# A mixer kernel on one Trainium2 core: batch 3's feature maps between the product reads of batch 1's block, and batch 0's last reads in another order

## The chip, the cores and the metric

The kernel runs on one core of a Trainium2 chip (trn2). The time is device microseconds (us) of one execution. Several runs are taken, and the median is given. Beside them there is one profiled execution, from which all rows of the trace come.

## What is computed

Eight batches of linear attention (8 heads, 576 positions, head size 64) are followed by a token-and-channel mixer.

```
phi(x) = where(x > 0, x, exp(x) - 1) + 1
kv = phi(k)^T v        z = sum over positions of phi(k)          per head
x  = (phi(q) kv) / (phi(q) z + 1e-6)                             576 x 512 per batch
u  = x + (relu(x^T w_tok1) w_tok2)^T                             token mixing, 576 -> 256 -> 576
out = u + relu(u w_ch1) w_ch2                                    channel mixing, 512 -> 1536 -> 512
```

Inputs and output are 32-bit floats. The matrix work inside is done in bfloat16.

## The kernel before, in words

**Tiling.** A batch has 576 positions: four row blocks of 128 and a tail of 64. The tails of two batches, 2p and 2p+1, share one block of 128 rows. The loaded q, k and v of a batch lie in `raw` buffers of two sets. Even batches and every batch from 2 on use set 0 and batch 1 uses set 1. After batch 1 the buffers of set 1 hold other things: sums of weights (`tb`, `tf`), sums of rows of the hidden layer (`sb`), and one of three parts of the output sum (`part`).

**One batch, stage by stage.**

- *Feature map.* phi is built as min(exp(x), max(x + 1, 1)). ScalarE does the exponential (`phi_exp`, L148), VectorE the add and max (`phi_add`, L154, into one of two buffers `y`) and the minimum (`phi_end`, L162, into `qp` or `kp`). Each step comes as two instructions of 128 x 1152, one for each half of the heads. The two ends of k are what `kv` (L188) waits for, with the cast of v (`vcast`, L173).
- *kv* is 72 small matmuls (L188). ScalarE copies the result out (L194). q is transposed by SyncE's transposing transfers (`qtr_dma`, L218).
- *Normalisation* (`nd_all`, L258 on TensorE; L267, L269, L271, L278 on VectorE) divides and gives x. It uses PSUM banks 2 to 7.
- *Token mixing* is `mm1` (L302, relu on ScalarE at L305) and `mm2` (L315). mm2 has two halves: mm2a gives rows 0 and 1 of u, mm2b rows 2 and 3. VectorE adds x (L327). Two transposing transfers on SyncE's queue (`utr_dma`, L510; called uta and utb) turn u into uT.
- *Channel mixing, first half* (`mm3`, L528) takes uT and makes the hidden layer `cr`, 12 column blocks of four matmuls. Each block has a PSUM bank that a tuple at L524 to L526 names. ScalarE (L535) or VectorE (L532) takes the relu. `mm3_tail` (L542, L544) does the same for the shared tail rows in three groups, with banks from the tuple at L538.
- *Channel mixing, second half.* Batches 1 to 6 use seven products in place of eight (`pair_product`, L690). A batch has 14 product steps (7 products, each for two row pairs) of 6 matmuls. The products are summed in three PSUM tiles X, Z and Y. Some need row sums of the hidden layer, which VectorE makes (`row_sums`, L625). ScalarE copies intermediate values of a tile out (`pair_copy`, L695). VectorE reads the tiles and adds u into the output buffer (`pair_end`, L701). GpSimd adds the copied parts (L703) and sends the result (L707). The tail rows are one product with `crt` (`mm4` with t = 8, L555, twelve matmuls).
- Batch 0 has no such products. Its second half (`mm4`, L555) sums in four held banks, t = 0 to 3, which the ring of banks puts in banks 2, 3, 0, 1. `mm4_end` (L572) reads each, adds u, and has GpSimd send two at a time (L577).

**Order.** Nothing is scheduled by a planner. The order on each engine is the order in which the program issues instructions. A block of batch n is a list `big` of steps of TensorE work, and a list `fill` of pairs (step, work), where the work is issued right after its step. In this way the work of batch n+1 (attention, token mixing) and the feature maps of batch n+2 stand between the matmuls of batch n. In batch 1's block, steps 0 to 11 are mm3, 12 to 14 mm3_tail, 15 to 28 the product steps, and 29 to 31 the tail product in groups of four matmuls. The products go in the order 1, 2, 6, 5, 7, 3, 4, so product step 17 is the first half of product 2, and 23 and 24 are product 7. kv of batch 3 stands behind step 29. Batch 2's block follows. It starts with mm3 of batch 2, which needs the whole of its uT.

**Queues.** SyncE's queue carries all loads (`load_all`, L129) and all transposing transfers in program order. A transfer that waits holds those behind it. GpSimd makes sums of weights early in batch 1's block (`weight_sums`, L611).

**Lines the change touches.** `mm3` L524 to L526, `mm3_tail` L538, `pair_product` L679, `pair_end` L697, the last `fill` of batch 0's block at L911 to L914, and the `put` list of batch 1's block at L931 to L975.

Of the kernel before, what the change touches and what calls it, by code (L numbers as in the profile page):

```python
# [18 lines left out]
def kernel(  # L19
# [26 lines left out]
    R = 4  # L46
# [18 lines left out]
    def bank(at=None):  # L65
        if at is None:
            at, ring[1] = ring[1], (ring[1] + 1) % 4
        return psum[:, at]
# [68 lines left out]
    live = {}  # L137
    o_at = [0]

    def o_slots(m):  # L140
        at = o_at[0] if o_at[0] + m <= 10 else 0
        o_at[0] = (at + m) % 10
        return obuf[:, at:at + m]
# [198 lines left out]
    def mm2_half(n, c):  # L342
        b = n % 2
        cs = COLS[c]
        for rs in ([0, 1], [2, 3]):
            ps = bank(4 + 2 * c + rs[0] // 2).rearrange(
                "p (r c) -> p r c", r=2)
            add = rs[0] == 0
            for i, r in enumerate(rs):
                if add:  # L350
                    nc.tensor.matmul(out=ps[:, i], lhsT=identity, rhs=x[b][:, r, cs],
                                     start=True, stop=False)
                for kt in range(NT):
                    nc.tensor.matmul(out=ps[:, i], lhsT=w2v(kt, r), rhs=ar[b][:, kt, cs],
                                     start=(kt == 0 and not add), stop=(kt == NT - 1))
            if add:
                nc.scalar.copy(out=u[b][:, 0:2, cs], in_=ps)
            else:
                nc.vector.tensor_tensor(out=u[b][:, 2:4, cs], in0=ps, in1=x[b][:, 2:4, cs],
                                        op=ALU.add)  # L360

    def utr(n, js):
        b = n % 2
        for jp in js:
            tp = bank(4 + 2 * jp).bitcast(BF16).rearrange("p (j r c) -> p j r c", j=2, r=R)
            for i in range(2):
                j = 2 * jp + i
                for r in range(R):
                    nc.tensor.transpose(out=tp[:, i, r, :],
                                        in_=u[b][:, r, 128 * j:128 * j + 128], identity=identity)  # L370
            for i, copy in enumerate((nc.scalar.copy, nc.vector.tensor_copy)):
                copy(out=uT[b][:, :, 2 * jp + i], in_=tp[:, i])
# [147 lines left out]
    def mm3(n, mc, kjs=range(NDM), dve=False):  # L520
        b = n % 2
        if kjs[0] == 0:
            part_of[mc] = bank(None if n == 0 else (
                (0, 1, 0, 1, 2, 3, 0, 1, 2, 3, 0, 1) if n > 1 else  # L524
                (3, 5, 7, 1, 3, 0, 2, 1, 3, 0, 1, 0))[mc])
        ps = part_of[mc]  # L526
        for kj in kjs:
            nc.tensor.matmul(out=ps, lhsT=wc1[:, kj, 128 * mc:128 * mc + 128],  # L528
                             rhs=uT[b][:, :, kj],
                             start=(kj == 0), stop=(kj == NDM - 1))  # L530
        if kjs[-1] == NDM - 1 and dve:
            nc.vector.tensor_scalar(out=cr[b][:, mc, :], in0=ps, scalar1=0.0, scalar2=None,  # L532
                                    op0=ALU.max)
        elif kjs[-1] == NDM - 1:
            nc.scalar.activation(out=cr[b][:, mc, :], in_=ps, func=AF.Relu)  # L535

    def mm3_tail(i, late=True):
        ps = bank(((2, 3, 0) if late else (1, 2, 3))[i]).rearrange("p (m s) -> p m s", m=4)  # L538
        for m in range(4):
            mc = 4 * i + m  # L540
            for kj in range(NDM):
                nc.tensor.matmul(out=ps[:, m], lhsT=wc1[:, kj, 128 * mc:128 * mc + 128],  # L542
                                 rhs=uTt[:, kj, :], start=(kj == 0), stop=(kj == NDM - 1))
        nc.scalar.activation(out=crt[:, 4 * i:4 * i + 4, :], in_=ps, func=AF.Relu)  # L544
# [18 lines left out]
    def mm4_end(p, t):  # L563
        ps = held[t]
        b, r = divmod(t, R)
        last = p == B // 2 - 1
        put = nc.sync if last else nc.gpsimd
        if t < 8:
            if last or r % 2 == 0:
                live["o"] = o_slots(2)  # L570
            o = live["o"][:, 0 if last else r % 2]
            nc.vector.tensor_tensor(out=o, in0=ps, in1=u[b][:, r, :], op=ALU.add)  # L572
            m = 1 if last else 2
            if r % m == m - 1:
                r0 = r - m + 1
                for e in range(2):
                    (nc.scalar if last and e else put).dma_start(  # L577
                        out=outv[2 * p + b, :, 2 * r0 + e:2 * r0 + e + 2 * m - 1:2],
                        in_=live["o"][half[e], 0:m])
        else:  # L580
            o = o_slots(2)[:, 0]
            nc.vector.tensor_tensor(out=o, in0=ps, in1=ut[p % 2], op=ALU.add)
            for b in range(2):
                (nc.scalar if last and b else put).dma_start(
                    out=outv[2 * p + b, :, 2 * R], in_=o[half[b]])
# [3 lines left out]
    KH = NCH // 2  # L589
# [11 lines left out]
    def wblock(i, j):  # L601
        return wc2[:, KH * i:KH * (i + 1), 256 * j:256 * (j + 1)]
# [76 lines left out]
    def pair_product(n, i, j):  # L679
        a_ = lambda h, e: ablock(n, h, e)[:, :, j]  # L680
        lhs, rhs, tile_, first = {
            1: (a_(0, 0), wblock(0, 0), "X", True), 2: (a_(1, 0), wblock(1, 0), "Z", True),
            6: (sb[1][:, :, j], tb[1], "X", False), 5: (sb[0][:, :, j], tb[0], "Y", True),
            7: (sb[2][:, :, j], tb[2], "X", False), 4: (a_(1, 1), tb[3], "X", False),
            3: (sb[3][:, :, j], wblock(1, 1), "Y", False)}[i]
        if first and j == 0:
            live[tile_] = bank({"X": 2 - n % 2, "Z": 2 * (n % 2), "Y": 3}[tile_]).rearrange(
                "p (j c) -> p j c", j=2)
        for k_ in range(KH):
            nc.tensor.matmul(out=live[tile_][:, j], lhsT=lhs[:, k_], rhs=rhs[:, k_],  # L690
                             start=(first and j == 0 and k_ == 0), stop=(k_ == KH - 1),
                             skip_group_check=not first or j == 1)
# [2 lines left out]
        nc.scalar.copy(out=part[i], in_=live["Y" if i == 2 else "X"])  # L695

    def pair_end(n, tile_, d, c, i=None):  # L697
        if tile_ == "Z":
            live["o4"] = o_slots(4)
        o = live["o4"][:, d::2, HC[c]]  # L700
        nc.vector.tensor_tensor(out=o, in0=live[tile_], in1=u[n % 2][:, d::2, HC[c]], op=ALU.add)  # L701
        if i is not None:
            nc.gpsimd.tensor_tensor(out=o, in0=o, in1=part[i], op=ALU.add)  # L703
# [132 lines left out]
    for mc in range(2):  # L836
        mm3(0, mc, range(0, 2))
# [66 lines left out]
    late = [("vc", lambda: vcast(1, 0)), ("vc", lambda: vcast(1, 1, nc.vector.tensor_copy))]  # L904
# [4 lines left out]
    for nm, fn in first[1:2] + late + first[2:3] + first[0:1] + first[3:]:  # L909
        fill += [(at0[nm], fn)]  # L910
    fill += [(23, fn) for fn in (  # L911
        lambda: mm4_end(0, 0), lambda: mm4_end(0, 1), lambda: mm2_half(1, 0),
        lambda: mm2_half(1, 1), lambda: utr(1, [0]), lambda: mm4_end(0, 2),
        lambda: mm2(1, [R]), lambda: utr(1, [1]), lambda: mm4_end(0, 3))]  # L914
    run(big, sorted(fill, key=lambda e: e[0]))


# [7 lines left out]
    put = lambda s, fn, *a: fill.append((s, lambda: fn(*a)))  # L925
    todo = dict(steps(2))
# [11 lines left out]
    put(5, vcast, 2, 1, nc.vector.tensor_copy)  # L938
    put(6, load_all, 3, "v")
    put(8, kv, 2, range(2))  # L940
    put(10, todo["nd"])
    for s, k0 in ((11, 0), (12, 3)):
        for w in (1, 2):
            put(s, row_sums, 1, w, k0, 3)
    for g in range(2):
        put(12 + g, phi_exp, "q", 3, 2 * g, 2)
        put(13, phi_add, "q", 3, 2 * g, 2)
        put(14, phi_end, "q", 3, 2 * g, 2)
    put(15, qtr_dma, 3)
    put(16, pair_copy, 0)  # L950
    put(16, todo["mm1"])
    put(17, row_sums, 1, 3, 0, KH)
    for g in range(2):
        put(17 + g, vcast, 3, g)
    put(19, todo["mm2a"])
    put(19, todo["uta"])
    put(20, row_sums, 1, 4, 0, KH)
    put(20, pair_copy, 1)
    put(21, pair_end, 1, "Z", 0, 0, 0)
    put(21, todo["mm2b"])  # L960
    put(21, todo["utb"])
    put(22, load_all, 4, "qv")
    put(22, pair_copy, 2)
    put(22, k_exp, 3)
    put(24, pair_end, 1, "X", 1, 1, 2)
    for g in range(2):
        put(24, phi_add, "k", 3, 2 * g, 2)
    put(25, load_all, 4, "k")
    put(26, pair_end, 1, "Y", 0, 1, 1)
    for g in range(2):  # L970
        put(27, phi_end, "k", 3, 2 * g, 2)
    put(28, pair_end, 1, "X", 1, 0)
    put(28, pair_put, 1)
    put(29, kv, 3, range(2))
# [2 lines left out]
    for n in range(2, B - 1):  # L977
        p, b = divmod(n, 2)
        big = m3(n) + (m3t if b else []) + m4s(n) + (m4(p, [8]) if b else [])
        b0 = 15 if b else 12  # L980
        todo = dict(steps(n + 1))
        fill = []
        put = lambda s, fn, *a: fill.append((s, lambda: fn(*a)))
# [93 lines left out]
```

## Time and profile before

| what | value |
|---|---|
| median of 11 runs | 256.1 us (254.62 to 256.45) |
| profiled execution, time | 256.15 us |
| profiled execution, span | 254.4 us |
| mean granted TensorE clock | 0.993 |
| TensorE matmul busy | 243.4 us, 96% |
| VectorE busy | 172.1 us, 68% |
| ScalarE busy | 141.1 us, 55% |
| GpSimd busy | 68.8 us, 27% |
| HBM traffic | 178 GB/s over the span |
| L690 products | 273 ns for one of 128 x 256, in 504 matmuls |
| L528 mm3 | 380 ns for one of 128 x 512, in 384 matmuls |

In a row of the timeline the columns are the start in us, the busy time in us, the engine, the line, the operation, output<-input, shapes and types, and the number of instructions. Brackets hold the idle time ahead of the row and what ended it. The duration of one matmul is longer than the distance to the next, since matmuls are pipelined: four mm3 matmuls, of 380 ns each, take 0.86 us in the chain of waits. Neighbouring rows of VectorE and ScalarE overlap by 0.03 to 0.1 us in the same way.

The chain of waits names, for every stretch of time, the work that ended last. TensorE has 85% of it, VectorE 6%, ScalarE 3%.

### The profile page before, as it was taken

To read this page: it belongs to the slowest core of one execution; us is meant where nothing else is said; L and a number is where in the kernel's file an instruction comes from. 1 tells how busy PE (TensorE), PEld (TensorE's weight loads), DVE (VectorE), ACT (ScalarE), POOL (GpSimd) and SP (SyncE) were. 2 spreads that over 40 slices of the span, in tenths; PEclk is the share of its full clock that TensorE was granted. 3 is DMA by queue.
4 is the path that set the end of the run, shared out by engine and by line. 5 is a ranking of instruction groups with operands and counts; after the bars stand their busy time and mean duration, and the time that the engine had idled before them with its cause. 6 is when DMAs were issued, how large, how long until landed. Compare 5 with 4: busy or idle time off the path is not lost.

```text
span 254.4 us, 5863 instructions
## 1 busy us (share of the span) xinstructions
PE 243.4 (96%) x2411; PEld 152.5 (60%) x2430; DVE 172.1 (68%) x296; ACT 141.1 (55%) x224; POOL 68.8 (27%) x80
## 2 busy tenths in 40 slices
PE   7899999999998799999999999999999999999993
PEld 3574455644876344774488545675588545764872
DVE  5955758796999476977685398948864353933543
ACT  4764871578764159655987268565863165127400
POOL 9670120597405310052002600051003500150000
PEclk9999999999999799999999999999999999999999
DMA  6999999899429970879938966669152440425034
GB/s 245 263 203 260 374 234 345 305 269 318 183 61 200 388 295 12 126 183 265 412 134 173 393 173 214 130 173 385 42 116 45 100 108 0 82 59 129 0 94 116
DMA packets 49707, 48.39 MB, mean 190 GB/s; under 512 B 30032, under 2 KB 35536, under 8 KB 49680
## 3 DMA queue, kind: packets, MB, share of 16 engines
q1 hardware_dynamic: 41568, 34.87, 45.9%
q0 software_dynamic: 7568, 12.49, 21.7%
q10 hardware_dynamic: 544, 0.66, 1.1%
q8 instruction: 19, 0.31, 0.5%
q14 instruction: 8, 0.07, 0.1%
HBM read 35.85 MB, written 9.44 MB: 178 GB/s over the span
## 4 chain that ended last, share of the span: by engine, by line
PE 85%; DVE 6%; ACT 3%; issue 3%; DMA 2%; DVEq 0%; ACTq 0%
PE ps L528 30%; PE ps L690 21%; PE ps L555 7%; PE ps L302 6%; PE ps L542 4%; PE ps L315 4%; PE ps L643 4%; DVE kp L162 2%; PE ps L188 2%; PE ps L258 2%; DMA k_raw<-in_k_dram 2%; DVE y L154 1%; PE ps L463 1%; ACT e L148 1%; PE ps L473 1%
## 5 line engine op out<-in xcount | busy, mean ns | idle before, releaser
L528 PE MATMUL ps<-uT,wc 128*128 128x512 bf16 x384 | 87.6, 380 | 0.0
L535 ACT ACTIVATE cr<-ps 128x512 bf16<-128x512 f32 x91 | 53.3, 600 | 44.5 <-PE ps L528 43.9
L528 PEld LDWEIGHTS <-wc 128*128 128x128 bf16 x384 | 36.9, 98 | 43.9 <-issue 2.5
L703 POOL TENSOR_TENSOR obuf<-obuf,q_raw 128x512 f32<-128x512 f32 x6 | 7.6, 1269 | 107.4 <-ACT w L695 76.9
L701 DVE TENSOR_TENSOR obuf<-ps,u 128x512 f32<-128x512 f32 x24 | 16.5, 689 | 14.3 <-PE ps L690 11.3
L690 PE MATMUL ps<-k_raw,v_raw 128*128 128x256 bf16 x216 | 25.4, 273 | 0.0
L625 DVE TENSOR_TENSOR v_raw<-cr 128x768 bf16<-128x768 bf16 (+1 forms) x21 | 14.4, 687 | 16.2 <-ACT cr L535 16.2
L690 PEld LDWEIGHTS <-v_raw 128*128 128x128 bf16 x216 | 20.9, 98 | 4.7 <-issue 1.2
L690 PEld LDWEIGHTS <-cr 128*128 128x128 bf16 x216 | 21.0, 98 | 4.3
L148 ACT ACTIVATE e<-q_raw 128x1152 bf16<-128x1152 f32 x16 | 18.2, 1159 | 6.9 <-DVE den L238 5.0
L148 ACT ACTIVATE e<-k_raw 128x1152 bf16<-128x1152 f32 x16 | 18.1, 1162 | 3.7 <-DMA k_raw<-in_k_dram 3.7
L690 PE MATMUL ps<-wc,cr 128*128 128x256 bf16 x144 | 17.7, 273 | 0.0
L271 DVE TENSOR_TENSOR x<-ps,dens 128x768 bf16<-128x768 f32 x18 | 17.2, 958 | 0.6
L327 DVE TENSOR_TENSOR u<-ps,x 128x1024 bf16<-128x1024 f32 x12 | 14.7, 1223 | 3.9 <-PE ps L315 3.6
L162 DVE TENSOR_TENSOR kp<-e,y 128x1152 bf16<-128x1152 bf16 x16 | 12.8, 818 | 2.8 <-ACT e L148 2.6
L162 DVE TENSOR_TENSOR qp<-e,y 128x1152 bf16<-128x1152 bf16 x16 | 11.9, 756 | 3.9 <-ACT e L148 3.0
L154 DVE TENSOR_SCALAR y<-k_raw 128x1152 bf16<-128x1152 f32 x16 | 12.7, 821 | 2.2 <-DMA k_raw<-in_k_dram 2.2
L302 PE MATMUL ps<-x,w 128*128 128x512 bf16 x49 | 13.8, 379 | 0.3
L173 ACT CAST vs<-v_raw 128x1152 bf16<-128x1152 f32 x12 | 13.4, 1162 | 0.0
L154 DVE TENSOR_SCALAR y<-q_raw 128x1152 bf16<-128x1152 f32 x16 | 12.1, 766 | 0.0
L315 PE MATMUL ps<-ar,w2p 128*128 128x512 bf16 x45 | 11.8, 379 | 0.3
L542 PEld LDWEIGHTS <-wc 128*128 128x128 bf16 x192 | 11.2, 98 | 1.4
(132 smaller groups left out, 347.4 us busy)
## 6 DMA issues: line engine op xcount, KB each, us to landing
k_raw<-in_k_dram SPq DMA_DIRECT2D x16, 576.0 KB, 6.6
q_raw<-in_q_dram SPq DMA_DIRECT2D x16, 576.0 KB, 6.2
v_raw<-in_v_dram SPq DMA_DIRECT2D x14, 576.0 KB, 8.3
out_dram<-obuf POOLq DMA_DIRECT2D x12, 512.0 KB, 7.0
wc<-in_moe_w_ch_dram POOLq DMA_DIRECT2D x8, 384.0 KB, 10.1
out_dram<-obuf POOLq DMA_DIRECT2D x4, 256.0 KB, 5.5
out_dram<-obuf POOLq DMA_DIRECT2D x6, 128.0 KB, 5.7
cr<-in_v_dram POOLq DMA_DIRECT2D x2, 288.0 KB, 7.7
```

The lines of the kernel that those rows point to most:

```text
L148: nc.scalar.activation(out=e, in_=f, func=AF.Exp)
L154: nc.vector.tensor_scalar(out=y, in0=f, scalar1=1.0, scalar2=1.0, op0=ALU.add, op1=ALU.max)
L162: live["phi"] = nc.vector.tensor_tensor(out=dst.transpose([0, 2, 1, 3]), in0=e.rearrange("p (i t d) -> p i t d", i=nj, t=T), in1=y.rearran ...
L271: nc.vector.tensor_tensor(out=xv[:, :, rc0:rc0 + 3], in0=v_[:, :, k0:k0 + 6, 0:D].rearrange("p i (q a) d -> p i q a d", a=2), in1=den[:, : ...
L302: nc.tensor.matmul(out=ps[:, mt], lhsT=w1t[:, b, ms] if r == R else w1[:, r, ms], rhs=x[b][:, r, :], start=(r == 0), stop=(r == R))
L315: nc.tensor.matmul(out=ps[:, i], lhsT=w2v(kt, r, b), rhs=ar[b][:, kt, :], start=(kt == 0), stop=(kt == NT - 1 and not add))
L528: nc.tensor.matmul(out=ps, lhsT=wc1[:, kj, 128 * mc:128 * mc + 128], rhs=uT[b][:, :, kj], start=(kj == 0), stop=(kj == NDM - 1))
L535: nc.scalar.activation(out=cr[b][:, mc, :], in_=ps, func=AF.Relu)
L542: nc.tensor.matmul(out=ps[:, m], lhsT=wc1[:, kj, 128 * mc:128 * mc + 128], rhs=uTt[:, kj, :], start=(kj == 0), stop=(kj == NDM - 1))
L555: nc.tensor.matmul(out=ps, lhsT=crt[:, kc, :] if t == 8 else cr[b][:, kc, 128 * r:128 * r + 128], rhs=wc2[:, kc, :], start=(kc == 0), stop ...
L690: nc.tensor.matmul(out=live[tile_][:, j], lhsT=lhs[:, k_], rhs=rhs[:, k_], start=(first and j == 0 and k_ == 0), stop=(k_ == KH - 1), skip ...
L701: nc.vector.tensor_tensor(out=o, in0=live[tile_], in1=u[n % 2][:, d::2, HC[c]], op=ALU.add)
```

## The change

All of it lies at the end of batch 0's block and in batch 1's block. No instruction is added or removed.

1. **End of batch 0's block.** The read of held tile 2 (`mm4_end(0, 2)`) moves from ahead of the small tail step `mm2(1, [R])` to behind the second uT copy. Reads 2 and 3 now stand together at the end.
2. **Banks.** In batch 1's mm3 the banks 0 and 1 change places where they occur from block 3 on, and mm3_tail takes banks 0, 2, 3 instead of 1, 2, 3.
3. **q of batch 3.** Both adds move from step 13 to step 9, ahead of the normalisation of batch 2. The second end of q goes from behind all of step 13 to step 14, still with no VectorE work between the two ends.
4. **k of batch 3.** Both adds move from step 24 to step 15. The two exponentials, both at step 22 before, go to step 17 (first half) and step 22 (second half). The two ends, both at step 27 before, go to step 20 and step 24.
5. **v of batch 3.** The cast of the second half moves from step 18 to step 22, behind k's second exponential.
6. **Sums.** Row sum 4 moves from step 20 to step 18.
7. **Reads and mm2b.** The read of tile Z moves from step 21 to step 24, behind the read of X. mm2b with utb, its transposing transfer, moves from step 21 to step 24, behind both reads.
8. **Loads of batch 4.** q and v moved from step 22, k from step 25; now all three are at step 25. Their order on SyncE's queue is unchanged.
9. The four output slots are taken at the first product step instead of at the read of Z.

On VectorE, the order from the second cast of v of batch 2 to the tail's read becomes: relu, q adds, normalisation, sums 1 and 2, q ends, k adds, sum 3, sum 4, u rows 0 and 1, both k ends, reads of X and Z, u rows 2 and 3, reads of Y and X. On GpSimd, the parts' adds of X and Z change places. On SyncE the order stays.

```diff
@@ mm3
-                (3, 5, 7, 1, 3, 0, 2, 1, 3, 0, 1, 0))[mc])
+                (3, 5, 7, 0, 3, 1, 2, 0, 3, 1, 0, 1))[mc])
@@ mm3_tail
-        ps = bank(((2, 3, 0) if late else (1, 2, 3))[i]).rearrange("p (m s) -> p m s", m=4)
+        ps = bank(((2, 3, 0) if late else (0, 2, 3))[i]).rearrange("p (m s) -> p m s", m=4)
@@ pair_product
+        if i == 1 and j == 0:
+            live["o4"] = o_slots(4)
@@ pair_end
-        if tile_ == "Z":
-            live["o4"] = o_slots(4)
@@ end of batch 0's block
-        lambda: mm2_half(1, 1), lambda: utr(1, [0]), lambda: mm4_end(0, 2),
-        lambda: mm2(1, [R]), lambda: utr(1, [1]), lambda: mm4_end(0, 3))]
+        lambda: mm2_half(1, 1), lambda: utr(1, [0]),
+        lambda: mm2(1, [R]), lambda: utr(1, [1]), lambda: mm4_end(0, 2), lambda: mm4_end(0, 3))]
@@ batch 1's block
     put(8, kv, 2, range(2))
+    for g in range(2):
+        put(9, phi_add, "q", 3, 2 * g, 2)
     put(10, todo["nd"])
...
     for g in range(2):
         put(12 + g, phi_exp, "q", 3, 2 * g, 2)
-        put(13, phi_add, "q", 3, 2 * g, 2)
-        put(14, phi_end, "q", 3, 2 * g, 2)
+        put(13 + g, phi_end, "q", 3, 2 * g, 2)
     put(15, qtr_dma, 3)
+    for g in range(2):
+        put(15, phi_add, "k", 3, 2 * g, 2)
     put(16, pair_copy, 0)
     put(16, todo["mm1"])
     put(17, row_sums, 1, 3, 0, KH)
-    for g in range(2):
-        put(17 + g, vcast, 3, g)
+    put(17, vcast, 3, 0)
+    put(17, phi_exp, "k", 3, 0, 2)
+    put(18, row_sums, 1, 4, 0, KH)
     put(19, todo["mm2a"])
     put(19, todo["uta"])
-    put(20, row_sums, 1, 4, 0, KH)
     put(20, pair_copy, 1)
-    put(21, pair_end, 1, "Z", 0, 0, 0)
-    put(21, todo["mm2b"])
-    put(21, todo["utb"])
-    put(22, load_all, 4, "qv")
+    put(20, phi_end, "k", 3, 0, 2)
     put(22, pair_copy, 2)
-    put(22, k_exp, 3)
+    put(22, phi_exp, "k", 3, 2, 2)
+    put(22, vcast, 3, 1)
+    put(24, phi_end, "k", 3, 2, 2)
     put(24, pair_end, 1, "X", 1, 1, 2)
-    for g in range(2):
-        put(24, phi_add, "k", 3, 2 * g, 2)
-    put(25, load_all, 4, "k")
+    put(24, pair_end, 1, "Z", 0, 0, 0)
+    put(24, todo["mm2b"])
+    put(24, todo["utb"])
+    put(25, load_all, 4, "qvk")
     put(26, pair_end, 1, "Y", 0, 1, 1)
-    for g in range(2):
-        put(27, phi_end, "k", 3, 2 * g, 2)
     put(28, pair_end, 1, "X", 1, 0)
```

## The prediction

> **What bounds the kernel now.** The page first: busy shares, then the 40 slices.
>
> ```profile
> PE 243.4 (96%) x2411; PEld 152.5 (60%) x2430; DVE 172.1 (68%) x296; ACT 141.1 (55%) x224; POOL 68.8 (27%) x80
> ...
> PE   7899999999998799999999999999999999999993
> ...
> PEclk9999999999999799999999999999999999999999
> ```
>
> TensorE carries the span, and after the start it is loose in one place only: the 13th and 14th slices (one is 6.36 us, so 76 to 89 us), and the 14th is the only one whose granted clock is under 9. That is the end of batch 1's block. So I asked for stages there (columns: stage, its length, then busy us and instructions of PE, PEld, DVE, ACT, POOL, then PEclk, DMA share, GB/s), and for TensorE's and VectorE's rows in order of time.
>
> ```profile
> 78.20:81.58 3.38, 3.32 (x27) 2.39 (x25) 3.38 (x4) 1.32 (x2) 1.64 (x1) 1.00 0.95 162
> 81.58:84.84 3.26, 0.97 (x72) 0.81 (x74) 3.26 (x4) 0.00 (x0) 1.71 (x1) 1.00 1.00 366
> 84.84:88.00 3.16, 3.00 (x9) 1.21 (x10) 0.06 (x1) 0.75 (x2) 1.26 (x2) 0.56 1.04 411
> 88.00:90.09 2.09, 2.09 (x13) 0.71 (x12) 0.69 (x1) 0.60 (x1) 1.07 (x2) 0.86 1.04 345
> ```
> ```profile
> 82.62 0.48 PE L188 MATMUL ps<-vs,kp 64*64 64x65 bf16 x36 [1.04 <-DVE kp L162]
> 84.36 0.48 PE L188 MATMUL ps<-vs,kp 64*64 64x65 bf16 x36 [1.26 <-DVE kp L162]
> 85.00 3.00 PE L555 MATMUL ps<-wc,crt 128*128 128x512 bf16 x7 [0.16 <-issue]
> ```
> ```profile
> 76.60 1.22 DVE L327 TENSOR_TENSOR u<-ps,x 128x1024 bf16<-128x1024 f32 x1
> 78.20 0.69 DVE L701 TENSOR_TENSOR obuf<-ps,u 128x512 f32<-128x512 f32 x1 [0.39 <-PE ps L690]
> 78.81 2.49 DVE L154 TENSOR_SCALAR y<-k_raw 128x1152 bf16<-128x1152 f32 x2
> 81.22 0.68 DVE L701 TENSOR_TENSOR obuf<-ps,u 128x512 f32<-128x512 f32 x1
> 81.82 2.48 DVE L162 TENSOR_TENSOR kp<-e,y 128x1152 bf16<-128x1152 bf16 x2
> 84.23 0.68 DVE L701 TENSOR_TENSOR obuf<-ps,u 128x512 f32<-128x512 f32 x1
> ```
>
> VectorE never pauses from 78.20 to 84.9: the feature map of k of batch 3 (two adds, L154, two ends, L162) comes last, and the kv product of batch 3 (L188), which stands in TensorE's order between the tail product's first four matmuls and its last eight, waits for it. TensorE loses 1.04 + 1.26 + 0.16 = 2.46 us. The clock then falls to 0.56: seven L555 take 3.00 us where seven at 0.216 take 1.51 (0.86 us for four is the chain's row elsewhere), a loss of 1.49, and the eight L528 of 88.00 take 2.09 instead of the chain's usual 1.73, a loss of 0.36. Together 4.3 us hang on this one wait. The four VectorE rows are also stretched: L154 and L162 take 1.42 for two at 70.28 and 71.61, but 2.49 and 2.48 here, while GpSimd's L703 runs (79.04 to 80.68, 81.98 to 83.69).
>
> **The change part by part.** TensorE's instructions stay the same, and in the same order but for one thing: the four matmuls of mm2b (rows 2, 3 of batch 2's token mixing, 0.86 us) move from behind product step 21 to behind step 24.
>
> *The feature maps.* q's two adds move ahead of VectorE's normalisation of batch 2 (L267 to L278), into the 2.21 us in which VectorE waits for L258 (61.52 to 63.72). There they meet GpSimd's weight sums (L611, until 66.42), and no L154 or L162 in the trace lies under an L611. Bounds: 1.42 us uncontended, 2.49 as beside L703. Taking 2.49, since this line's only contended row is that one and L173 beside the same L611 also grew from 0.76 to 1.40: 61.44 + 2.4 = 63.85, against a start at 63.72, so 0.13 late. Here the Trainium skill speaks against the change: "SBUF — State Buffer", section "SBUF: two separate sides", says that VectorE and GpSimd share one port pair as an exclusive lock held for a whole instruction. By it each add may wait out an L611 of about 1.15 us: two of (1.15 + 0.67) end at 65.1, and the normalisation is 1.35 late. Its first part then frees PSUM bank 2 at 65.36 + 1.35 = 66.7, where the second group of mm3_tail wants it at 65.87: 0.8 us lost on TensorE. By the rows the loss is nothing (65.36 + 0.13). I take the rows.
>
> k's adds move to right behind q's ends (GpSimd idle there: 66.4 to 76.8), k's first end behind u's rows 0 and 1, k's second end ahead of the reads of the products. VectorE from the normalisation's end, back-to-back spacing from the rows (L625 pairs 2.12 for four, L154 and L162 0.67, L625 of 1536 0.87, L327 1.14, L701 0.61): 68.16 + 2.12 (sums 1, 2) + 1.34 (q ends) + 1.34 (k adds) + 0.87 + 0.87 (sums 3, 4) = 74.70; L327 for mm2a (its matmuls end at 73.95) to 75.84; k's first end to 76.51. This costs nothing on the path: sums 3 and 4 feed product steps 23 and 25, at 76 us and later, and u's rows 0, 1 leave 0.7 us later for a batch that starts at 84.
>
> *ScalarE.* The second exponential of k stands behind part copy 2 (L695), that is behind product step 22. Without mm2b in front, step 22 ends at 73.95 + 18 x 0.1093 = 75.92 (54 products take 5.90 us); copy 0.03 + 0.58; exponential 1.12: 77.65. The second vs cast (1.1) ends at 78.8, needed at 82. So k's second end waits on VectorE from 76.51 to 77.70 and holds it; that is the new wait, and queued behind it are all four reads of the products and u's rows 2, 3. It swallows any lateness up to 1.2 us from above.
>
> *Reads and mm2b.* k end 77.70 + 0.67; L701 for X and Z + 1.22 = 79.59; L327 for mm2b + 1.24 = 80.83 (mm2b's matmuls are over at 78.1). Bank 2, for the tail product, is free at 79.7, needed at 80.72; banks 4 and 5, for kv, at 80.83, needed at 81.58. The other two L701 end by 82.1. GpSimd's three L703 no longer meet a two-operand SBUF operation of VectorE, so k's ends cost 0.67 each.
>
> *SyncE.* The transposing transfer of u rows 2, 3 (L510) issues at 80.83, not 77.84: 3 us later. It landed 3.0 to 4.7 us after issue, the one here in 3.1: uT is whole at 83.95. Before, nothing waited for it (TensorE reached mm3 at 87.8). Behind it on the same queue go the six loads of batch 4, about 3 us later than now.
>
> *TensorE.* From 73.95: 54 product matmuls 5.90, mm2b 0.86, twelve L555 2.59, kv 0.71: mm3 of batch 2 can start at 84.01, with uT there at 83.95. I allow 0.1 for the hand-over. Eight L528 at 1.73 bring it to 85.84, where the trace of before has 90.09: 4.25 us gained. With kv's end at 78.4 and cover of 3 us, the 2.46 us wait is gone; what is late next is uT, a dead heat.
>
> *End of batch 0's block.* The read of held bank 0 (L572) moves behind the small ut and uT steps; the banks in mm3 and mm3_tail are renamed to suit. TensorE gets mm3 of batch 1 some 0.4 us sooner (L504 no longer waits for a read of 0.69), but kv of batch 2 waits for VectorE's L173 anyway (0.34 us now), and VectorE does the same work: I count one hand-over saved, 0.1. At most the 0.34 comes.
>
> Sum: 4.25 + 0.1 = 4.35; the profiled execution took 256.15 us (span 254.4), so 251.8. The median of the runs is 256.1: the same.
>
> **Does the clock come with it?** "TensorE: Matmul & The Clock Gate", section "Why this matters for your kernels", allows gaps up to about 3 us before the clock is halved. The longest gap here is 1.26 us, all three 2.46: by the rule the gap would not halve it, and removing it might give only 2.46 + 0.1, so 253.6. But the row shows 0.56 directly behind a stage with 0.97 us of small matmuls in 3.26 us, and 1.00 in every other stage of 20 us that I asked for. I take the row.
>
> **The rivals.**
> - *uT decides.* A landing of 4.7 instead of 3.1, or a later exponential, makes TensorE wait 1 to 1.6 us at 84: 252.8 to 253.4; if the clock falls with it (1.85), up to 255.3. For it: the dead heat. Against: nothing else is on the queues then, and it landed in 3.0 to 3.5 in most blocks. 14%.
> - *The clock falls anyway*: 253.6. 6%.
> - *The port lock bites at L611*: 252.6. 6%.
> - *The wait stays in another dress*: kv waits for the vs cast or k's end because ScalarE runs 4 us late: about 256. Against: 3 us of cover. 3%.
> - *Slower: batch 4's k comes too late.* Its loads issue at 84.4 to 85.4; before they took 9.6 and 12.8, so up to 98 us. VectorE's add of it would come at 100.02 - 4.35 = 95.7 and stand in front of batch 2's row sums and u. Up to 2.5 us late is free (the sums end at 103.57, product 6 starts at 106.06). It decides only when it eats 4.35 + 0.77: landing 18 us after issue; 257. Against: the longest row is 12.8, with more traffic in front. 5%.
>
> **How the numbers follow.** The likeliest, 66%: 251.8, own range 251.3 to 252.4. A measurement of this kernel can tell about 0.3%, 0.77 us, from no change. Faster takes the likeliest and the first three rivals less the worst of the first: 0.91; same 0.04; slower 0.05. The range: below, 251.0 (all of the 0.34, and a few tenths of spread, for three of the 11 runs lie 1.3 us under the median); above, 253.6, which takes in the clock and the late uT.
>
> **What would show it.** In the profile after: L188 of batch 3 with no wait for L162; PEclk 1.00 through 80 to 90; L154 for q at 61.4 (1.4 to 2.5 for two); L162 for k waiting on L148 at about 77.7; the second L510 at about 80.8; mm3 of batch 2 near 84.1; nothing longer behind it. I am wrong if L528 waits for the transfer by more than half a microsecond, if the clock still falls, or if L154 for k near 95.7 waits for its load.

## The result, and the profile after

The changed kernel takes 253.05 us (median of 12 runs, 252.57 to 253.47). The kernel before takes 255.81 us (47 runs, 254.25 to 256.45, with the 11 shown above among them). The ratio is 0.9905, with a 95% interval of 0.9885 to 0.9925, so the change is a gain of about 1%. The forecast was 251.8, with a range of 251.0 to 253.6. The side and the range were right, but the gain is 2.76 us and not 4.35. Of the 1.59 us between them, 1.25 is the changed kernel (253.05 against 251.8), and 0.34 is the kernel before, whose profiled execution took 256.15 where its median is 255.81.

The profiled execution of the changed kernel took 253.29 us, with a span of 251.5. The page's slices show the weak place closed: the 13th and 14th digits are 9, and so is the clock of the 14th.

```profile
PE 240.9 (96%) x2411; PEld 151.9 (60%) x2430; DVE 171.3 (68%) x296; ACT 141.3 (56%) x224; POOL 68.7 (27%) x80
...
PE   7789999999999999989999999999999999999993
...
PEclk9999999999999999999999999999999999999999
```

The timeline of the same place, TensorE's rows first (start, busy time, engine, line, operation, shapes, number, idle time ahead). In the changed kernel two lines go in at L686 and two go out behind, so L690 of before is L692 here, L695 is L697, and L701 stays.

```profile
82.08 0.78 PE L188 MATMUL ps<-vs,kp 64*64 64x65 bf16 x72
83.01 1.67 PE L555 MATMUL ps<-wc,crt 128*128 128x512 bf16 x7 [0.16 <-issue]
84.45 1.47 PEld L528 LDWEIGHTS <-wc 128*128 128x128 bf16 x8 [0.25 <-DMA uT<-u]
84.52 1.89 PE L528 MATMUL ps<-uT,wc 128*128 128x512 bf16 x8
```
```profile
61.93 2.75 DVE L154 TENSOR_SCALAR y<-q_raw 128x1152 bf16<-128x1152 f32 x2
...
78.21 0.76 DVE L162 TENSOR_TENSOR kp<-e,y 128x1152 bf16<-128x1152 bf16 x1 [0.77 <-ACT e L148]
78.88 1.28 DVE L701 TENSOR_TENSOR obuf<-ps,u 128x512 f32<-128x512 f32 x2
80.08 1.22 DVE L327 TENSOR_TENSOR u<-ps,x 128x1024 bf16<-128x1024 f32 x1
```

kv of batch 3 is one piece of 72 matmuls with no wait. The seven L555 behind it take 1.67 us instead of 3.00. q's adds are stretched under L611, k's second end waits for ScalarE's exponential, and uT arrives just as TensorE gets to mm3: the weight load of mm3 waited 0.25 us, but the matmuls themselves follow L555 without a gap. All of this was forecast.

What was not: farther on, in batch 2's block, a new wait.

```profile
97.05 0.76 DVE L154 TENSOR_SCALAR y<-k_raw 128x1152 bf16<-128x1152 f32 x1 [0.62 <-DMA k_raw<-in_k_dram]
...
98.85 0.76 DVE L154 TENSOR_SCALAR y<-k_raw 128x1152 bf16<-128x1152 f32 x1 [1.04 <-DMA k_raw<-in_k_dram]
...
109.01 1.29 DVE L701 TENSOR_TENSOR obuf<-ps,u 128x512 f32<-128x512 f32 x2
...
109.75 1.47 PE L692 MATMUL ps<-q_raw,cr 128*128 128x256 bf16 x12 [0.66 <-DVE obuf L701]
```

The load of batch 4's k lands at 98.8 us, and VectorE's add waits for it twice. That is one of the prediction's own signs of being wrong (L154 for k waits for its load). The chain of waits then runs from that load through VectorE's queue, with no idle stretch over 0.6 us, to product 4, which must not write tile X before L701 has read it. Product 4 starts 2.14 us behind the start of product 3 (107.61), where it was 1.32 in the kernel before (111.29 to 112.61):

```profile
86.20 12.56 DMA k_raw<-in_k_dram
...
98.85 0.76 DVE y L154
...
102.79 0.95 DVE v_raw L625
103.74 1.34 DVE kp L162 x2
105.08 1.14 DVE u L327
106.21 0.82 DVE q_raw L625
...
109.01 0.70 DVE obuf L701
109.71 0.04 issue
109.75 1.47 PE ps L692 x12
```

**Where the time went.** I count between fixed points of TensorE's program: the first matmul of batch 1's second token mixing (L351, ahead of all that the change touches), the normalisation of batch 3 (L258) and mm3 of batch 3 (L528).

| us | before | after | difference |
|---|---|---|---|
| start to L351 | 48.20 | 48.69 | +0.49 |
| L351 to L258 of batch 3 | 41.82 | 37.66 | -4.16 |
| L258 to L528 of batch 3 | 23.90 | 24.71 | +0.81 |
| from there to the end of the span | 140.48 | 140.44 | -0.04 |

The first row is no effect of the change: the program up to there is the same, and over all twelve profiles of this study it varies from 48.05 to 48.98. The second row is the forecast gain (4.35 was predicted). The third holds the wait of product 4; e1 below ties it to the late k.

**The median of before is a mixture.** The 58 runs of the kernel before that were taken beside the experiments below, on three chips, fall into two groups by their mean granted clock: 31 runs at 0.990 to 0.993 take 256.10 us (median), 27 at 0.996 to 1.000 take 254.45. The profiled execution of before is of the first group. Its fall by itself (0.56 over 3.16 us and 0.86 over 2.09 us) makes a mean of 0.993 over the span of 254.4 us, by estimate from these rows. A run's mean doesn't say where the clock fell, but the changed kernel, without this wait, has all its 12 runs at 0.996 or above, and so has e2 below, in which the wait is filled. So the clock falls at this wait in about half of the executions. Against the runs of before that kept the clock, the change gives only 1.4 us (254.45 to 253.05). The rows would make it 1.7 (2.46 and 0.1, less the 0.83 that e1 gives for the late k); the other 0.3 is open.

### The profile page after: what moved, and what is told of

It is laid out like the page before. It is cut to its first block, busy times and chain, and to the rows that moved or that the text cites. A ratio compares the mean times of both kernels' runs of the same rounds, so it can differ in the third digit from the quotient of the medians.

```text
span 251.5 us, 5859 instructions
## 1 busy us (share of the span) xinstructions
PE 240.9 (96%) x2411; PEld 151.9 (60%) x2430; DVE 171.3 (68%) x296; ACT 141.3 (56%) x224; POOL 68.7 (27%) x80
## 4 chain that ended last, share of the span: by engine, by line
PE 68%; DMA 14%; DVE 8%; POOL 3%; ACT 3%; issue 2%; SPq 1%; DVEq 0%; POOLq 0%; ACTq 0%
PE ps L528 22%; PE ps L692 19%; PE ps L555 6%; DMA k_raw<-in_k_dram 5%; DMA q_raw<-in_q_dram 5%; PE ps L302 5%; PE ps L542 4%; DMA wc<-in_moe_w_ch_dram 4%; PE ps L643 4%; PE ps L315 3%; PE ps L188 2%; PE ps L258 1%; SPq L129 1%; DVE v_raw L625 1%; DVE kp L162 1%
## 5 line engine op out<-in xcount | busy, mean ns | idle before, releaser
L528 PE MATMUL ps<-uT,wc 128*128 128x512 bf16 x384 | 87.2, 379 | 0.0
L528 PEld LDWEIGHTS <-wc 128*128 128x128 bf16 x384 | 36.7, 98 | 43.3 <-issue 1.5
L703 POOL TENSOR_TENSOR obuf<-obuf,q_raw 128x512 f32<-128x512 f32 x6 | 7.6, 1268 | 97.8 <-ACT w L697 76.8
L701 DVE TENSOR_TENSOR obuf<-ps,u 128x512 f32<-128x512 f32 x24 | 16.3, 688 | 13.4 <-PE ps L692 8.6
L692 PE MATMUL ps<-k_raw,v_raw 128*128 128x256 bf16 x216 | 25.2, 273 | 0.0
L692 PEld LDWEIGHTS <-cr 128*128 128x128 bf16 x216 | 21.0, 98 | 5.1 <-issue 0.8
L692 PEld LDWEIGHTS <-v_raw 128*128 128x128 bf16 x216 | 20.9, 98 | 4.5 <-issue 1.2
L692 PE MATMUL ps<-wc,cr 128*128 128x256 bf16 x144 | 17.7, 273 | 0.0
L162 DVE TENSOR_TENSOR kp<-e,y 128x1152 bf16<-128x1152 bf16 x16 | 11.8, 752 | 3.6 <-ACT e L148 3.4
L154 DVE TENSOR_SCALAR y<-k_raw 128x1152 bf16<-128x1152 f32 x16 | 11.7, 754 | 3.3 <-DMA k_raw<-in_k_dram 3.3
L154 DVE TENSOR_SCALAR y<-q_raw 128x1152 bf16<-128x1152 f32 x16 | 13.4, 850 | 0.6 <-DMA q_raw<-in_q_dram 0.6
L173 ACT CAST vs<-v_raw 128x1152 bf16<-128x1152 f32 x12 | 13.5, 1160 | 0.0
L703 POOL TENSOR_TENSOR obuf<-obuf,part 128x512 f32<-128x512 f32 x6 | 7.6, 1269 | 18.1 <-DVE obuf L701 18.1
```

The source lines that it names most:

```text
L154: nc.vector.tensor_scalar(out=y, in0=f, scalar1=1.0, scalar2=1.0, op0=ALU.add, op1=ALU.max)
L162: live["phi"] = nc.vector.tensor_tensor(out=dst.transpose([0, 2, 1, 3]), in0=e.rearrange("p (i t d) -> p i t d", i=nj, t=T), in1=y.rearran ...
```

## The experiments

My theory after the result: the gain at the wait came as forecast, and 0.8 us went to the late k of batch 4. The rivals: VectorE's new order costs by itself, the clock's part was mis-sized, or the edits ahead of the gap cost something.

Since the start of the program spreads by 0.9 us, I give beside each median the profiled execution's time from L351 to the normalisation of batch 3 and to mm3 of batch 3. These were 41.82 and 65.72 before, and 37.66 and 62.37 after. I call them the anchored times; each comes from one profile. The experiments ran on three chips, each beside runs of the kernel before; the ratios are to these.

**e1: the loads in another order.** On the changed kernel:

```diff
-    put(25, load_all, 4, "qvk")
+    put(25, load_all, 4, "qkv")
```

> The changed kernel with one edit: batch 4's loads are queued in the order q, k, v instead of q, v, k. Theory: in the changed kernel k of batch 4 lands at 98.8 us, VectorE's add (L154) waits 0.62 + 1.04 us for it, everything behind it on VectorE runs 1.7 us late, and TensorE waits about 0.8 us for the read of X (L701) in batch 2's block. With k second it lands before 97, so no wait for the load and no wait of product 4: 0.7 to 0.9 us below the changed kernel, about 252.2 us. Rival: the late TensorE wait comes from VectorE's own order in the earlier start, not from the load; then the time stays at 253.0. Second rival: v, now last, makes the cast late and with it kv of batch 4: 253 or more.

Measured: 251.89 us (251.76 to 252.47), ratio to before 0.9866 (0.9837 to 0.9896); 37.65 and 61.54. The adds run back to back, and product 4 waits for nothing:

```profile
96.16 1.42 DVE L154 TENSOR_SCALAR y<-k_raw 128x1152 bf16<-128x1152 f32 x2
```
```profile
108.74 1.47 PE L692 MATMUL ps<-q_raw,cr 128*128 128x256 bf16 x12
```

The 0.83 us between the two anchored times (62.37 to 61.54) is the price of the late k in these profiles. The medians differ by 1.16. The other 0.33 can be the spread of the start, or a k that comes later still in other executions (in e4's profile product 4 waits 1.14 us); no run separates the two. The first rival falls. So does the second: v is queued last, and its cast (L173, at 104.08) waits for nothing. This version beats both kernels, and its median is within 0.1 of the forecast of 251.8.

**e6: k's adds behind the row sums.** On the changed kernel, whose loads stay in the order q, v, k:

```diff
-            if n == 2:
-                for g in range(2):
-                    put(10, phi_add, "k", n + 2, 2 * g, 2)
...
+        if n == 2:
+            for g in range(2):
+                put(12, phi_add, "k", n + 2, 2 * g, 2)
```

> The changed kernel with its own load order q, v, k, and one edit in batch 2's block: the two adds of batch 4's k (L154) stand behind row sums 1 and 2 on VectorE instead of ahead of them. The load still lands at about 98.8 us. Theory (it is not the landing but the place of the waiting add at the head of VectorE's queue that costs): the sums fill the wait, the queue behind is 1.7 us less late, TensorE's wait for X goes, about 252.0 us as with e1. Rival: k's ends and kv of batch 4 depend on the late load anyway, and the time stays near 253.0.

Measured: 252.3 us (252.14 to 252.53), 0.9871 (0.9849 to 0.9893); 37.65 and 61.82. The load is no faster: its second half lands 13.6 us after its issue, where it was 12.6 in the changed kernel. But the add no longer waits, because the row sums stand ahead of it:

```profile
98.76 0.56 DVE L625 TENSOR_TENSOR v_raw<-v_raw,cr 128x768 bf16<-128x768 bf16 x1
99.24 1.42 DVE L154 TENSOR_SCALAR y<-k_raw 128x1152 bf16<-128x1152 f32 x2
```

0.55 of the 0.83 us come back. So it is the place of the waiting add at the head of VectorE's queue that costs, and most of the cost goes without any faster load. The last 0.28 stay, since VectorE is late all the same: it reads X at 107.93, and product 4 starts at 108.67, 1.59 us behind product 3 instead of 1.32.

**e2: the wait kept, the clock held.** On the kernel before, nine matmuls are added in the wait. They write an unused bank, and nothing reads them.

```diff
+            if fill:
+                for _ in range(fill[c]):
+                    nc.tensor.matmul(out=psum[:, 6], lhsT=wc1[:, 0, 0:128], rhs=wc2[:, 0, :],
+                                     start=True, stop=True)
...
-    put(29, kv, 3, range(2))
+    put(29, kv, 3, range(2), (4, 5))
```

> The kernel before with nine added matmuls of 128 x 512 into an unused PSUM bank, four ahead of the first half and five ahead of the second half of kv of batch 3, where TensorE waits for VectorE. Their result is not read. The wait itself stays. Theory (the row of the trace): the halved clock after the wait comes from TensorE being nearly empty over 3.3 us. With filler the granted clock stays at 1.00 and about 1.8 us come back: 254.0 to 254.4 us. Rival (the rule taken by its words): gaps of 1.26 us don't halve the clock, so it falls for another reason; then nothing comes back: 255.8, or a little more for filler that overshoots.

Measured: 254.46 us (22 runs, 254.17 to 254.92), 0.9962 (0.9945 to 0.9979); 40.13 and 64.03. In this run's kernel kv is L192, and L188 is the filler. The two halves of kv start at 82.64 and 84.38, as before (82.62 and 84.36):

```profile
82.64 0.49 PE L192 MATMUL ps<-vs,kp 64*64 64x65 bf16 x36 [0.18 <-DVE kp L162]
83.06 1.25 PE L188 MATMUL ps<-wc,wc 128*128 128x512 bf16 x5
84.38 0.48 PE L192 MATMUL ps<-vs,kp 64*64 64x65 bf16 x36
```

In the stages (columns as in the prediction, the clock third from the right) the wait is filled and the clock stays, where one row of before has 0.50:

```profile
86.00:87.00 1.00, 1.00 (x4) 0.36 (x3) 0.00 (x0) 0.00 (x0) 0.73 (x2) 0.50 1.06 417
```
```profile
81.58:84.84 3.26, 3.02 (x82) 1.40 (x81) 3.26 (x4) 0.00 (x0) 1.71 (x1) 1.00 0.96 346
84.84:88.00 3.16, 3.00 (x18) 1.43 (x16) 0.78 (x2) 1.16 (x3) 1.55 (x3) 1.00 1.04 405
```

1.69 us come back in the anchored time (1.85 were read from the rows of before), and the median is that of the runs of before that kept their clock (254.45). The rule taken by its words falls here: a TensorE with 0.97 us of work in 3.26 us lost its clock in about half of the executions, though the longest gap is 1.26 us. How little filler would do was not tried. What e1 has over this kernel, 254.46 to 251.89, is 2.57 us by the medians and 2.48 in the anchored time (40.13 to 37.65). That is the whole rearrangement with the clock held on both sides; the wait was read as 2.46, and the end of batch 0's block as 0.1.

**e3: the end of batch 0's block alone.** On the kernel before, parts 1 and 2 of the change (the read of held tile 2 and the banks; diff as above).

> The kernel before with the first two parts of the change alone: the read of held tile 2 behind the second uT copy, and the renamed banks of mm3 and mm3_tail. Theory: TensorE reaches kv of batch 2 sooner and waits there for VectorE's cast (L173), whose time does not move: 0 to 0.1 us, so 255.8, no difference that can be measured. Rival: VectorE's order saves more and the cast comes sooner: up to 0.34 us less.

Measured: 255.89 us, 0.9997 (0.9972 to 1.0023); 41.70 and 65.59, so 0.12 less in the anchored time. kv of batch 2 starts sooner and its second half waits for the cast, as predicted:

```profile
61.03 0.48 PE L188 MATMUL ps<-vs,kp 64*64 64x65 bf16 x36 [0.34 <-DVE vs L173]
```

**e4: q's adds back.** On the changed kernel:

```diff
-        put(9, phi_add, "q", 3, 2 * g, 2)
+        put(13, phi_add, "q", 3, 2 * g, 2)
```

> The changed kernel with q's two adds back at step 13, behind the normalisation and sums 1 and 2. Theory: the early place of q's adds meets GpSimd's weight sums (2.75 us for two instead of 1.42) and delays the normalisation by 0.4 us, which costs TensorE nothing; back at step 13 they take 1.42 us on VectorE ahead of k's ends, of which about 0.4 + 0.8 are covered by the earlier normalisation and by VectorE's wait for ScalarE. u rows 2 and 3 come 0 to 0.3 us later, mm3 of batch 2 starts 0 to 0.3 us later: 253.0 to 253.4 us. Rival (the port lock costs): the normalisation's lateness does cost, and the time falls below 252.8.

Measured: 253.32 us (252.85 to 254.34), 0.9924 (0.9894 to 0.9954); 37.68 and 63.19. The adds take 1.42 us and the gap's end stands where it stood in the changed kernel (37.66). So neither the stretch by GpSimd nor the earlier place costs or gives anything up to the normalisation of batch 3. The 0.8 us more at mm3 of batch 3 are put down to the load of k, which in this profile came later still (its second half landed 14.0 us after its issue; VectorE waited 1.71 and 0.75 us for it, and product 4 waited 1.14). That is one profile, and why the load took longer in it is not shown. The median lies 0.3 above the changed kernel, inside the spread of both.

**e5: the second exponential later.** On e1:

```diff
-    put(22, phi_exp, "k", 3, 2, 2)
     put(22, vcast, 3, 1)
+    put(22, phi_exp, "k", 3, 2, 2)
```

> The kernel of e1 (changed kernel, loads q, k, v) with one edit: ScalarE does the second cast of v ahead of k's second exponential, so the exponential ends 1.1 us later, and with it k's second end, the reads of X and Z, u rows 2 and 3 and their transposing transfer. Theory (mm3 of batch 2 stands in a dead heat with uT): each us of lateness costs TensorE a us; mm3 of batch 2 waits 1.0 to 1.3 us for the transfer, and the clock holds, because kv and the tail product stand just ahead of the wait: 252.9 to 253.2 us. Rival: there is slack that I did not see, under 252.3. Second rival: the wait of over 1 us takes the clock down as in the kernel before: 254 or more.

Measured: 253.22 us (253.1 to 254.7), 0.9923 (0.9893 to 0.9952); 38.63 and 62.52, so 0.98 more than e1. The size is about as expected and the clock holds (0.997 or above in all six runs). The place is not quite: product 4 of batch 1 waits first, for the read of X behind k's end, and uT second.

```profile
79.13 0.76 DVE L162 TENSOR_TENSOR kp<-e,y 128x1152 bf16<-128x1152 bf16 x1 [1.83 <-ACT e L148]
...
80.54 1.49 PE L692 MATMUL ps<-q_raw,cr 128*128 128x256 bf16 x12 [0.70 <-DVE obuf L701]
...
85.35 1.41 PEld L528 LDWEIGHTS <-wc 128*128 128x128 bf16 x8 [0.42 <-DMA uT<-u]
```

Two of the six runs took 254.5 and 254.7 with a full clock. I have no cause for them.

**e8: mm2b back at step 21.** On e1:

```diff
     put(20, phi_end, "k", 3, 0, 2)
+    put(21, pair_end, 1, "Z", 0, 0, 0)
+    put(21, todo["mm2b"])
+    put(21, todo["utb"])
...
-    put(24, pair_end, 1, "Z", 0, 0, 0)
-    put(24, todo["mm2b"])
-    put(24, todo["utb"])
```

> The kernel of e1 with the read of Z, mm2b and its transposing transfer back at step 21 as in the kernel before; the feature maps stay in their new places. Theory: the early feature maps alone remove the wait of kv of batch 3; moving mm2b behind the reads buys nothing and only made uT late. k's second end then comes at about 79, still over 2 us ahead of kv: 251.7 to 252.0, no difference from e1. Rival: with mm2b at step 21 the second exponential and k's end come late or meet GpSimd's adds (L703), and kv waits again: over 252.4.

Measured: 252.87 us (252.71 to 253.07), 0.9894 (0.9869 to 0.9918); 38.57 and 62.46, 0.92 more than e1. My theory missed, and of the rival only a part came: kv waits for nothing. Product 4 waits 0.75 us for the read of X:

```profile
76.74 0.59 ACT L697 COPY part<-ps 128x512 f32<-128x512 f32 x1 [1.59 <-PE ps L692]
77.22 1.17 ACT L148 ACTIVATE e<-k_raw 128x1152 bf16<-128x1152 f32 x1
77.53 1.27 POOL L703 TENSOR_TENSOR obuf<-obuf,q_raw 128x512 f32<-128x512 f32 x1 [10.22 <-DVE obuf L701]
78.44 0.98 DVE L162 TENSOR_TENSOR kp<-e,y 128x1152 bf16<-128x1152 bf16 x1
79.34 1.27 DVE L701 TENSOR_TENSOR obuf<-ps,u 128x512 f32<-128x512 f32 x2
80.07 1.48 PE L692 MATMUL ps<-q_raw,cr 128*128 128x256 bf16 x12 [0.75 <-DVE obuf L701]
```

mm2b ahead of step 22 makes part copy 2 on ScalarE later by its 0.86 us (from L351 it starts at 28.69, in e1 at 27.83), then the exponential, k's second end, and the read of X queued behind it. k's end also takes 0.98 us instead of 0.76, beside GpSimd's L703: the contention that the rival named is some 0.2 us of this.

**e9: X read ahead of k's second end.** On e8:

```diff
-    put(24, phi_end, "k", 3, 2, 2)
     put(24, pair_end, 1, "X", 1, 1, 2)
+    put(24, phi_end, "k", 3, 2, 2)
```

> The kernel of e8 (loads q, k, v; mm2b and the read of Z back at step 21) with one edit: VectorE reads X before k's second end instead of behind it. Theory formed from e5 and e8: what cost e8 about 0.9 us is that the read of X stands behind k's second end, which waits for ScalarE, and product 4 cannot write X before it is read. With X first, product 4 waits for nothing, k's second end comes at about 79.5, kv at about 81.5, so nothing waits: 251.8 to 252.1 us, as e1. Rival: mm2b in its old place costs by itself (GpSimd's adds against k's end, ScalarE's part copy), and the time stays over 252.6.

Measured: 251.93 us (251.75 to 252.76), 0.9881 (0.9849 to 0.9912); 37.66 and 61.56, the same as e1. Product 4 starts as soon as X is read, and without a wait:

```profile
79.00 0.68 DVE L701 TENSOR_TENSOR obuf<-ps,u 128x512 f32<-128x512 f32 x1
79.60 0.75 DVE L162 TENSOR_TENSOR kp<-e,y 128x1152 bf16<-128x1152 bf16 x1
```
```profile
79.74 1.48 PE L692 MATMUL ps<-q_raw,cr 128*128 128x256 bf16 x12
```

So mm2b's old place costs nothing when X is read first, and moving it buys nothing. It matters only where k's end stands ahead of the read of X.

**e7: the sums of weights later.** On e1, with the first of the last six L611 made to wait for the cast (L173) instead of for k's end:

```diff
-        first = [live["phi"]]
+        first = [live["cast" if "late" in live else "phi"]]
...
-    put(3, weight_sums, (tf, B22, tf), (tb[3], B21, tf))
...
     put(5, vcast, 2, 1, nc.vector.tensor_copy)
+    put(5, live.__setitem__, "late", True)
+    put(5, weight_sums, (tf, B22, tf), (tb[3], B21, tf))
```

> The kernel of e1 with GpSimd's last six sums of weights (L611) started behind VectorE's cast of v of batch 2 (L173) instead of ahead of it. Theory: the cast then takes 0.76 us instead of 1.40, and TensorE's 0.34 us wait ahead of the second half of kv of batch 2 goes; q's adds are stretched as before or more. 0.3 to 0.5 us below e1: 251.4 to 251.6. Rival: GpSimd ends later (68 to 69 us), ScalarE's first part copy, which writes over the same buffer, waits for it, and the gain is lost: 251.9 or more.

Measured: 252.08 us (251.32 to 252.34, 5 runs), 0.9853 (0.9826 to 0.988); 37.28 and 61.18. The cast is short, kv of batch 2 runs in one piece, and 0.36 us are gained in the anchored time:

```profile
60.29 0.74 DVE L173 CAST vs<-v_raw 128x1152 bf16<-128x1152 f32 x1
60.92 0.78 PE L188 MATMUL ps<-vs,kp 64*64 64x65 bf16 x72
```

The median doesn't show it, and lies above what I expected. The profiled run's L351 started at 48.98, the latest of all, 0.47 behind e1's, but that is one run of the five. On the runs alone, e7 against e1 is inconclusive.

**e10: e9 and e7 together.**

> The kernel of e9 with e7's edit too: GpSimd's last six sums of weights behind VectorE's cast of v of batch 2. Theory: the two waits are independent, so from the first step of batch 0's token mixing in halves (L351) to mm3 of batch 3 it takes 61.2 us as in e7, against 61.5 in e1 and 65.7 before: 251.4 to 251.8 us, with 0.5 us of spread from the start of the program. Rival: the later sums delay q's and k's feature maps and with X first k's end is too late for kv: 252 or more.

Measured: 251.79 us (251.5 to 252.06), 0.9868 (0.9835 to 0.99); 37.31 and 61.21. So e7's saving comes on top of e9 as it did on top of e1: 0.35 us in the anchored time. By the medians, e1, e9 and e10 cannot be told apart.

## Why the prediction was right in its side and wrong in its size

- *The gap and the clock.* Right. The stage gave 4.16 us in the profiled execution against 4.35 in the sum. The rearrangement with the clock held is 2.48 (e1 against e2, anchored) and the clock 1.69 (e2), against 2.56 (the wait and 0.1 for batch 0) and 1.85. Not foreseen: the clock falls in only about half of the runs, so the profiled execution of before shows more to gain than the runs do on average. The two groups stood in the 11 runs shown, and I took them for spread; the prediction also counted three runs 1.3 us under the median where there are two (254.62 and 254.83).
- *The clock rule.* The trace of before was the better guide. The Trainium skill's page "TensorE: Matmul & The Clock Gate" describes a window of 3.4 us (section "What's actually happening": it runs freely and doesn't start with the kernel). That would agree with a fall in 31 of 58 executions; no run here shows the window itself. The page's advice on single gaps, up to about 3 us, does not fit a fall behind gaps of 1.26 us at most.
- *q's adds and the port lock.* 2.75 us for the two, against 2.49 by the row and 3.6 by the prediction's estimate from the Trainium skill's page "SBUF — State Buffer" (two of 1.15 + 0.67). The row was nearer. The normalisation came 0.4 us later (64.60, where L258 at 63.71 would have let it start at 64.2), and that cost nothing (e4).
- *k's second end waits for ScalarE.* Right: VectorE had 0.77 us of wait there (1.2 forecast). The sum overlooked that product 4 needs the read of X behind it. It held by 0.2 us (the read ended at 79.57, product 4 started at 79.81), and e5 and e8 show what it costs when it doesn't.
- *uT in a dead heat.* Right: uT landed, and L528 started at 84.52, which is 84.01 plus the 0.49 of the start.
- *The end of batch 0's block.* 0.12 in e3 against 0.1.
- *The step that failed* in the size is in the rival "batch 4's k comes too late": "Up to 2.5 us late is free (the sums end at 103.57, product 6 starts at 106.06)". Its landing was forecast as up to 98 us and came at 98.8, of which 0.49 is the later start: that term held. But the slack was measured at the wrong consumer. VectorE's queue behind the add has one wait of 0.35 us up to the read of X, and product 4 stands 0.64 us behind the end of that read (111.97 to 112.61). Both stood in the trace of before:

```profile
103.92 1.23 DVE L327 TENSOR_TENSOR u<-ps,x 128x1024 bf16<-128x1024 f32 x1 [0.35 <-PE ps L315]
...
111.28 0.69 DVE L701 TENSOR_TENSOR obuf<-ps,u 128x512 f32<-128x512 f32 x1
```
```profile
112.61 1.47 PE L690 MATMUL ps<-q_raw,cr 128*128 128x256 bf16 x12
```

An add 1.85 us late (ended at 99.61; in e1 at 97.58, or 97.76 on this time base) cost 0.83, so about 1.0 us was free, which is 0.64 + 0.35, and not 2.5. I priced this mechanism at zero below a threshold that was too high, and so left 0.8 us out of the likeliest case.

- *The range held in part by luck.* 253.05 lies outside the likeliest case's own range (251.3 to 252.4). The upper end, 253.6, was set for a late uT and a fallen clock, and neither came; the late k, which did, was given no share in it.

What is left between the two profiled executions, 0.49, is the start: 4.16 - 0.81 - 0.49 = 2.86, which is 256.15 - 253.29.

## What to carry to other kernels

When work moves earlier, follow every queue that it was moved past to its last consumer, and look for the tightest one: here a transfer 1.85 us late at the head of VectorE's queue was passed on through ten microseconds of other work to a tile that TensorE wanted back. An operation that may wait for a load should stand behind the work that others wait for, or its load should be queued first. The slack of a late transfer is the sum of the waits on its way and the gap at that consumer, here 0.35 and 0.64 us. A kernel whose runs fall into two groups deserves a look at the granted clock of each run before the profiled execution is taken as typical.

## What the runs showed of the hardware

- TensorE's granted clock fell to 0.50 behind a stretch of 3.26 us with 0.97 us of 64 x 65 matmuls, though no gap was longer than 1.26 us (the profile of before). In 31 of 58 runs of that kernel the mean clock was 0.990 to 0.993. Nine matmuls of filler kept it at 1.00 in the profile and at 0.997 or above in all 22 runs.
- VectorE's 32-bit to 16-bit cast and add of 128 x 1152 take 0.74 to 0.76 us alone and 1.25 to 1.5 us each while GpSimd adds from SBUF. Moving GpSimd's work by 1.3 us took the cast from 1.40 to 0.74 (e7).
- Six loads of 576 KB, issued one behind the other beside 1.3 MB of stores, were complete 15.8 and 16.1 us after the first issue in the two kernels, 79.17 to 95.0 and 82.65 to 98.8 us. With k second instead of last (e1) its add waited for nothing. In the order q, v, k the last half of k took 12.6, 13.6 and 14.0 us from issue to landing in three profiles (changed kernel, e6, e4).
